# The order of small evictions in a fused attention and two-layer MLP kernel

## The chip, the cores and the metric

The kernel runs on one core of a Trainium2 chip. The metric is the device time of one execution in microseconds (us), the median over several runs. TensorE (PE in the profile) multiplies matrices into PSUM; VectorE (DVE), ScalarE (ACT) and GpSimd (POOL) work on tiles; SyncE (SP) issues the transfers. Each engine runs its own queue of instructions in order, and waits where an instruction needs another engine's result or has to leave a tile alone until another engine has read it.

## The reference

Causal attention with a decay, over 4 batches, 8 heads, 576 positions and 64 columns per head, and then two MLP layers over the 2304 tokens, all in float32:

```python
scores = scale * q @ k.T + decay                 # causal, per head
attn   = exp(scores - max) / (sum + 1e-9)
x      = (attn @ v) as 2304 tokens x 512
x      = (h - tanh(h)) @ w_out,   h = x @ w_in   # layer one, 512 -> 2048 -> 512
out    = relu(h)**2 @ w_out,      h = x @ w_in   # layer two, 512 -> 2048 -> 512
```

## The kernel before

**Numbers in two parts.** Most products are made from values split into a high part (fp32r, written by ScalarE) and a low part (the value minus its high part, written by VectorE). A product is then three matmul passes: high times high, high times low, low times high. So each value that PE reads first has one ScalarE instruction and one VectorE instruction behind it, and VectorE's can't begin before ScalarE's has ended.

**How the order is made.** A `Clockwork` object counts ticks. `cw.step(fn)` runs one piece of PE work and then whatever has come due; `cw.later(k, fn)` puts the eviction or split that follows on a heap, due k ticks later (the lags stand in `LAG`). What is written first has the higher priority, and a planner turns that into the queues of the engines. From the last block of layer one up to the tenth group of layer two, instructions that go through `pin` are kept strictly in the order in which they were written. The order in which instructions are written is also the order of the data: an instruction that writes a tile after another was written to read it waits for that read, and the other way round.

**Attention, second half.** The positions 256 to 575 of each head run as units n = 32 to 63, two neighbouring units (an even and an odd one) sharing a batch; PE alternates their pieces with matmuls of layer one. The softmax weights of a tile are turned by PE (`pt_atom`, L775), evicted as a high part into `PT[0]` (ACT, L784) three ticks later, and as a low part into `PT[1]` (DVE, L785) another two ticks later. `pv_atoms` then runs the product with the values in two passes: pass 0 reads `PT[0]` and pass 1 reads `PT[1]` (PE, L858). Both units of a pair use one copy of `PT[0]` and `PT[1]`, and they overlap in it: an odd unit's tile 2 lies where the even unit's tile 3 was.

**Last block of layer one.** Sixteen steps, each with 12 matmuls h (L1017) and 12 matmuls y (L1057) of 512 columns. An h is turned into g by a tanh (ACT, L1027), a difference (DVE, L1030), a high part (ACT, L1034) and a low part (DVE, L1038), and y of a step follows h of the next. Beside it the weights of layer two's first matrix are decoded, eight pieces p one after another (`decode_w`, `combine`, `split_all`); GpSimd makes sums of quarters (L256) and of inputs (L1186), and each piece has four splits, ACT high (L320) and DVE low (L321).

**Layer two's second matrix.** 36 groups n, each with 7 products of 6 matmuls (L1394). A group's inputs are loaded (`g_load`), squared (`g_square`, ACT L1336), combined by three differences and sums (`g_adds`, DVE L1344 to L1346) and split into a high part (`g_split`, ACT L1356) and a low part (`g_low`, DVE L1360), which PE reads. The table `AT` says before which product of group n the parts of a later group are written: before product 0 the high part of n + 2 and the differences of n + 3, then the low part of n + 2 before product 1, a load before product 3 and a square before product 5.

Of the kernel before, what the change touches and what calls it, by code (L numbers as in the profile page):

```python
# [10 lines left out]
F32 = mybir.dt.float32  # L11
# [3 lines left out]
ALU = mybir.AluOpType  # L15
# [3 lines left out]
B, H, S, D = 4, 8, 576, 64  # L19
NT, DM, DFF = B * S, H * D, 2048  # L20
P = 128
# [36 lines left out]
LAG = dict(max=2, exp=1, norm=3, tr=3, trlo=2, pv=1, pvadd=1, qk=1, qklo=1, th=1, sub=1, hi=1, lo=1, wbits=2, wparts=3,  # L58
           relu=1, sq=1, lo2=1, load=8)
# [51 lines left out]
def fused_kernel(ctx: ExitStack, tc: tile.TileContext, q, k, v, f, w1i, w1o, w2i, w2o, out):  # L111
    nc = tc.nc
# [33 lines left out]
    def pin(ins):  # L146
        if ordered:
            tc.keep_in_program_order(ins)
# [30 lines left out]
    def decoded():  # L179
        busy.pop()  # L180
        if pending:
            decode_w(*pending.pop(0))
# [130 lines left out]
    def split_all(phase, p, work, lag, at=None):  # L313

        def one(x):
            t, k, n, src = work[x]
            f = src.shape[-1]
            hi, lo = (t[:, hl, k : k + n].rearrange("p k f -> p (k f)").rearrange("p (c f) -> p c f", f=f)
                      for hl in range(2))
            pin(nc.scalar.activation(hi, src, AF.Copy))  # L320
            low = nc.vector.tensor_tensor(lo, in0=src, in1=hi.bitcast(F32), op=ALU.subtract)  # L321
            if phase == 2:
                pin(low)
            if x + 1 < len(work):
                if at is None:
                    cw.later(lag[x], lambda: one(x + 1))
            else:
                ready_w.add((phase, p))
                if phase == 1:
                    decoded()  # L330

        one(at or 0)

# [413 lines left out]
    def pt_atom(i):  # L747

        n, ts = slots[i]
        pb = Pb[i % RING]  # L750

        def a():
            while i not in ready_p:
                cw.step()
            if i == 0:
                keep_warm(WARM)
            t = bank("a", 4, f"pt_{i}")
            if len(ts) > 1:
                for x, (o, c) in enumerate(((0, 0), (128, 0), (128, 1))):
                    nc.tensor.transpose(t[:, x * P : x * P + P], pb[:, o + c * P : o + c * P + P], ident)  # L760
                cw.later(LAG['tr'], lambda: nc.scalar.activation(ptf(n), t[:, 0 : 3 * P], AF.Copy))
                return
            if not PT:
                for x in range(2):
                    PT.append(ap.tile([P, 1536], F32R, tag=f"PT{x}", name=f"PT{x}", bufs=1))
                PT.append(ap.tile([P, 2, P], F32R, tag="xq", name="PT4", bufs=1)[:, 0])
            ti = ts[0][0]
            if ti == 4:
                t4 = bank("a", 4, f"pt4_{i}")
                nc.tensor.transpose(t4[:, :P], pb[:, 512:640], ident)  # L770
                cw.later(LAG['tr'], lambda: last_keys(t4))
            nch = min(ti + 1, 4)
            for x in range(nch):
                s0 = (nch - 1 - x) * P
                nc.tensor.transpose(t[:, x * P : x * P + P], pb[:, s0 : s0 + P], ident)  # L775
            if ti == 4:
                src = t.rearrange("p (c h r) -> p c h r", c=4, h=2)
                dst = [each4(PT[x]) for x in range(2)]
            else:
                src = t[:, 0 : nch * P].rearrange("p (c r) -> p c r", c=nch)  # L780
                dst = [strided(PT[x], *PTC[n % 2][ti]) for x in range(2)]

            def ev():
                nc.scalar.activation(dst[0], src, AF.Copy)  # L784
                cw.later(LAG['trlo'], lambda: nc.vector.tensor_tensor(dst[1], src, dst[0].bitcast(F32), op=ALU.subtract))  # L785
            cw.later(LAG['tr'], ev)

        def last_keys(t4):
            nc.scalar.activation(PT[2], t4[:, :P], AF.Copy)
            x = PT[2][D:]  # L790
            cw.later(LAG['trlo'], lambda: nc.vector.tensor_tensor(x, t4[D:, :P], x.bitcast(F32), op=ALU.subtract))
        return 2 * sum((ti + 1) * rows for ti, rows, _, _ in ts), a

    def strided(t, d0, m):
# [3 lines left out]
    def each4(t):  # L798
        x = t[:, 0:D]
        return bass.AP(tensor=x.tensor, offset=x.offset, ap=[x.ap[0], [384, 4], [320, 2], [1, D]])  # L800

    ready_p = set()
    xs_box = {}
# [43 lines left out]
    def pv_atoms(n):  # L847
        b, hf, h = units[n]
        hh = h % 2
        nq = NQ[1]  # L850
        box = {}

        def a(hl):
            if hl == 0:
                box["t"] = bank("a", 4, f"pv_{n}")
            t = box["t"]
            for c, (c0, ql, w) in PVC[hh].items():
                nc.tensor.matmul(t[:, ql : ql + w], lhsT=VH[:, hh, c].rearrange("p a d -> p (a d)"),  # L858
                                 rhs=PT[hl][:, c0 : c0 + w], start=hl == 0 and c == 0, stop=False)
            if hl == 1:  # L860
                ql = 256 - 256 * hh
                nc.tensor.matmul(t[:, ql : ql + D], lhsT=VH[:, hh, 4].rearrange("p a d -> p (a d)"),
                                 rhs=PT[2][:, D - D * hh : 2 * D - D * hh], start=False, stop=True)
                cw.later(LAG['pv'], ev)

        def ev():
            t = box["t"]
            if hh == 0:
                xs_box["t"] = ap.tile([P, 320], F32, tag="xs", name=f"xs_{n}", bufs=2)
            xs = xs_box["t"]  # L870
            own = slice(hh * D, hh * D + D)
            oth = slice(D - hh * D, 2 * D - hh * D)
            tmp = ap.tile([P, 320], F32, tag="xtmp", name=f"xt_{n}", bufs=1)
            nc.scalar.activation(tmp[own, :nq], t[oth, :nq], AF.Copy)

            def fin():
                for c0, d0, w in ((0, 0, nq),) if hh == 0 else ((D, P, P), (D + P, 0, P), (0, 256, D)):
                    nc.vector.tensor_tensor(xs[own, d0 : d0 + w], t[own, c0 : c0 + w], tmp[own, c0 : c0 + w], op=ALU.add)
                if hh == 1:
                    pair_done(b, hf, h // 2, xs)  # L880
            cw.later(LAG['pvadd'], fin)

        cost = sum(max(256, w) for _, _, w in PVC[hh].values())
        return [(cost, lambda: a(0)), (cost + 256, lambda: a(1))]
# [230 lines left out]
    class Feed:  # L1115
# [11 lines left out]
        def one(self):  # L1127
            assert self.decoded < self.loaded
            decode_w(*self.items[self.decoded])
            self.decoded += 1  # L1130
# [138 lines left out]
    def put(g, dst):  # L1269
        move(dst, g.rearrange("p (b n) -> p b n", b=3))  # L1270

    def layer1():
        n = len(units1)
        for s in range(n):
            if s == 0:
                load_w(2, 0)
            if s < NP2:
                feed.upto(NF + s + 1)
            for pos, (d, k) in enumerate(STEP):
                if s == 0 and (d or k in PRE):  # L1280
                    continue
                due_at(7 * s + pos)
                cw.step(lambda: l1_product(s - d, k))
                feed.pace(NF + NP2)
        for at, (fn, x, k) in enumerate(((l2_product, 0, 1), (l2_product, 0, 6), (l1_product, n - 1, 4),
                                         (l2_product, 0, 7), (l1_product, n - 1, 3)), 7 * n):
            due_at(at)
            cw.step(lambda: fn(x, k))
# [45 lines left out]
    def g_square(n):  # L1334
        raw = graws[n][:, 0:4].rearrange("p k e t -> p (k e t)")
        pin(nc.scalar.activation(raw, raw, AF.Square))  # L1336
# [61 lines left out]
            cw.later(1, lambda: after2(j, k))  # L1398

    CALM = 10  # L1400
    AT = {0: ((g_split, 2), (g_adds, 3)), 1: ((g_low, 2),), 3: ((g_load, 5),), 5: ((g_square, 4),)}
    LATE = {(0, 4): (6, 0), (1, 4): (6, 1), (2, 4): (6, 2), (2, 6): (7, 0), (3, 4): (7, 1), (4, 2): (7, 2)}
    tmp2, outs2 = {}, {}
# [43 lines left out]

    def layer2():
        third()
        g_square(3)  # L1450
        g_load(4)
        g_load(5)
        for n in range(NG):
            if n == CALM:
                ordered.clear()
            for x, k in enumerate(ORDER2):
                for fn, m in AT.get(x, ()):
                    if n + m < NG and (fn is not g_square or n + m > 3) and (fn is not g_load or n + m > 5):
                        fn(n + m)
                if (n, x) in LATE:  # L1460
                    final_piece(*LATE[n, x])
                if n == 0 and x < 3:
                    continue
                cw.step(lambda: l2_product(n, k))
# [93 lines left out]
```

## Time and profile before

| | us |
|---|---|
| median of 3 runs (lowest to highest) | 1010.33 (1009.06 to 1011.22) |
| the profiled execution | 1005.81 |
| its span | 1004.1 |
| PE busy | 977.4 |
| DVE busy | 722.0 |
| ACT busy | 627.1 |
| POOL busy | 356.3 |

The span is the stretch from the first to the last instruction of the profiled execution. Busy is the time in which an engine had an instruction running; the ends of matmuls are modelled, so that neighbouring matmuls overlap a little in the rows.

### The profile page before, as it was taken

Reading aid. Unit: us, or ns where it says so; the run is one execution under the profiler, and the core shown is the slowest. Engines: PE = TensorE matmul, PEld = TensorE weight load, DVE = VectorE, ACT = ScalarE, POOL = GpSimd, SP = SyncE. Lnnn points to the kernel's source line nnn. Section 1 sums busy time; section 2 is a strip of 40 time slices with the busy share of each in tenths; the row PEclk is TensorE's granted clock in tenths of the full one; section 3 lists DMA queues with packets and bytes.
Section 4 is the critical chain, followed back from the end, with each engine's and each line's share of the span. In section 5 each row is a group of like instructions: output and inputs, shape, how many; then the busy total and the mean of one; then the engine's idle time right before and its main releaser. Section 6 shows DMA issues by size and latency. Waiting matters only on the chain.

```text
span 1004.1 us, 19916 instructions
## 1 busy us (share of the span) xinstructions
PE 977.4 (97%) x6990; PEld 929.5 (93%) x6990; DVE 722.0 (72%) x1513; ACT 627.1 (62%) x1249; POOL 356.3 (35%) x511
## 2 busy tenths in 40 slices
PE   7989999999999999999999999999999999999998
PEld 5778889999999999999999877999999999999998
DVE  4897884587878877878753589755447569987773
ACT  5896874566666666665643367767666767655551
POOL 4664453455566655565510343342323000000000
PEclk9999999999999999999999999999999999999999
DMA  8946744363353444443201432576877974544431
GB/s 235 272 137 228 217 112 100 107 140 82 101 142 91 115 120 102 113 120 93 75 20 36 153 127 84 162 258 222 282 272 247 331 229 118 168 141 134 127 106 42
DMA packets 220004, 149.58 MB, mean 149 GB/s; under 512 B 116384, under 2 KB 197600, under 8 KB 219904
## 3 DMA queue, kind: packets, MB, share of 16 engines
q1 hardware_dynamic: 219856, 148.28, 50.3%
q8 instruction: 55, 0.90, 0.4%
q14 instruction: 45, 0.37, 0.1%
q10 hardware_dynamic: 48, 0.03, 0.0%
HBM read 101.00 MB, written 39.92 MB: 140 GB/s over the span
## 4 chain that ended last, share of the span: by engine, by line
PE 68%; DVE 10%; ACT 3%; issue 2%; DMA 1%; SPq 1%; POOL 1%; DVEq 0%; ACTq 0%; POOLq 0%
PE o L1394 17%; PE r L1226 15%; PE h L1017 14%; PE y L1057 14%; PE pv L858 3%; PE pt L775 2%; DVE KL L630 2%; PE s L740 2%; DVE PT L785 2%; PE s L742 1%; DVE Pb L669 1%; DVE g L1030 1%; DVE ghl L1038 1%; DVE wq L321 1%; PE pv L820 1%
## 5 line engine op out<-in xcount | busy, mean ns | idle before, releaser
L1057 PE MATMUL y<-ghl,w 128*128 128x256 f32 (+1 forms) x1536 | 241.2, 301 | 1.5 <-DVE ghl L1038 1.5
L1057 PEld LDWEIGHTS y<-ghl,w 128*128 128x128 f32 x1536 | 209.5, 191 | 13.4 <-DVE ghl L1038 3.3
L1017 PE MATMUL h<-x,w 128*128 128x256 f32 x1344 | 199.2, 291 | 5.5 <-POOL w L228 4.7
L1017 PEld LDWEIGHTS h<-x,w 128*128 128x128 f32 x1344 | 175.9, 192 | 12.8 <-POOL w L228 6.3
L1394 PE MATMUL o<-ws,gc 128*128 128x256 f32 x864 | 116.0, 283 | 0.0
L1394 PEld LDWEIGHTS o<-ws,gc 128*128 128x128 f32 x864 | 109.2, 192 | 0.0
L1226 PE MATMUL r<-yt,ws 128*128 128x384 f32 x576 | 106.6, 336 | 0.5 <-ACT g L1244 0.5
L1226 PEld LDWEIGHTS r<-yt,ws 128*128 128x128 f32 x576 | 100.0, 188 | 2.9 <-ACT g L1244 2.5
L1394 PE MATMUL o<-wq,gc 128*128 128x256 f32 x648 | 90.9, 284 | 1.7 <-DVE gc L1360 1.5
L694 POOL TENSOR_SCALAR Pb<-Pb,st 128x384 f32<-128x384 f32 (+2 forms) x80 | 58.0, 726 | 81.1 <-DVE st L688 60.7
L1394 PEld LDWEIGHTS o<-wq,gc 128*128 128x128 f32 x648 | 83.5, 192 | 2.5 <-DVE gc L1360 1.9
L669 DVE CUSTOM_DVE_ANT_0 Pb<-s,Pb 128x128 f32<-128x128 f32 (+4 forms) x144 | 66.9, 482 | 22.1 <-PE s L742 13.8
L678 ACT ACTIVATE Pb<-Pb,st 128x384 f32<-128x384 f32 (+2 forms) x80 | 55.2, 689 | 42.8 <-DVE st L669 42.0
L1226 PE MATMUL r<-yt,wq 128*128 128x384 f32 x432 | 80.1, 335 | 0.3 <-ACT g L1244 0.2
L1030 DVE TENSOR_TENSOR g<-h,g 128x512 f32<-128x512 f32 x72 | 49.4, 686 | 42.5 <-ACT g L1027 41.8
L1360 DVE TENSOR_TENSOR gc<-graw,gc 128x1792 fp32r<-128x1792 f32 x34 | 68.7, 2022 | 13.5 <-ACT gc L1356 13.5
L1226 PEld LDWEIGHTS r<-yt,wq 128*128 128x128 f32 x432 | 75.1, 188 | 1.3 <-ACT g L1244 1.1
L1356 ACT ACTIVATE gc<-graw 128x1792 fp32r<-128x1792 f32 x34 | 57.7, 1697 | 28.0 <-PE o L1394 17.6
L256 POOL TENSOR_TENSOR wsum<-wfull 128x256 f32<-128x256 f32 x32 | 29.9, 935 | 118.5 <-DVE wfull L212 95.3
L1237 DVE TENSOR_TENSOR g<-r,g 128x384 f32<-128x384 f32 x71 | 39.0, 553 | 42.3 <-PE r L1226 23.3
L1027 ACT ACTIVATE g<-h 128x512 f32<-128x512 f32 x72 | 42.7, 592 | 40.2 <-PE h L1017 39.6
L1034 ACT ACTIVATE ghl<-g 128x512 fp32r<-128x512 f32 x72 | 45.4, 630 | 34.6 <-DVE g L1030 33.9
(155 smaller groups left out, 1879.1 us busy)
## 6 DMA issues: line engine op xcount, KB each, us to landing
graw<-gscr SPq DMA_DIRECT2D x144, 128.0 KB, 2.6
gscr<-g SPq DMA_DIRECT2D x95, 192.0 KB, 3.6
wraw<-in_moe_w_in_dram SPq DMA_DIRECT2D x32, 512.0 KB, 4.6
wraw<-in_moe_w_out_dram SPq DMA_DIRECT2D x32, 512.0 KB, 5.5
neg<-cscr SPq DMA_DIRECT2D x32, 288.0 KB, 3.4
v<-in_v_dram SPq DMA_DIRECT2D x48, 128.0 KB, 2.8
qk<-in_k_dram SPq DMA_DIRECT2D x64, 72.0 KB, 2.4
K<-K SPq DMA_DIRECT2D x32, 144.0 KB, 3.0
```

The costliest lines, as they stand in the source:

```text
L669: nc.vector.tensor_tensor_reduce(out=d, in0=t[:rows, src : src + m], in1=d, scale=-0.125, scalar=3.0e38 if j == 0 else stat(0, x)[:rows], ...
L678: nc.scalar.activation(d, d, AF.Exp, bias=stat(len(parts) - 1, x)[:rows], scale=-1.0, accum_out=stat(2, x)[:rows])
L694: nc.gpsimd.tensor_scalar(d, d, r, 1.0, op0=ALU.mult, op1=ALU.mult)
L1017: nc.tensor.matmul(o, lhsT=win(fc, wh, dc), rhs=xpart(j, dc, xh), start=dc == 0 and wh + xh == 0, stop=dc == ND - 1 and wh == 1)
L1027: pin(nc.scalar.activation(g, t, AF.Tanh))
L1030: pin(nc.vector.tensor_tensor(g, t, g, op=ALU.subtract))
L1034: pin(nc.scalar.activation(ghl[:, 0], g, AF.Copy))
L1057: nc.tensor.matmul(o, lhsT=wout(fc, wh, i * P, P), rhs=ghl[:, xh, fj * n : fj * n + n], start=s == 0 and fj == 0 and wh + xh == 0 and i % ...
L1226: nc.tensor.matmul(t, lhsT=wprod(1, p, k, wh)[:, dc * P : (dc + 1) * P], rhs=yt[i, k][:, xh, dc], start=k in FRESH and dc == 0 and wh + xh ...
L1356: pin(nc.scalar.activation(hi, t[:, 1:8], AF.Copy))
L1360: pin(nc.vector.tensor_tensor(lo, in0=t[:, 1:8], in1=hi.bitcast(F32), op=ALU.subtract))
L1394: nc.tensor.matmul(o, lhsT=gc[n][gh, e][:, GWHERE[k]] if n == 1 else gc[n][gh][:, GWHERE[k], e], rhs=wprod(2, 2 * q + e, k, wh), start=q = ...
```

## The change

It has three parts.

1. In the second half of attention, an eviction of turned weights is written only once the pass that reads the same buffer for the unit before it has been written (`behind`), and a pass is written only once all evictions that it reads have been (the loop over `need`, which lets ticks go by without PE work).
2. In layer two's opening groups, a table `OPEN` replaces `AT` for n = 0 and 1: `g_square(3)` moves from ahead of the loop to behind `g_split(2)`; `g_adds(3)` moves behind `g_low(2)`; `g_square(4)` and `g_adds(4)` move behind `g_low(3)`.
3. In the last block, the low parts of layer two's first weights are written two ticks after their high parts instead of together with them, and are pinned; the piece counts as ready, and the next one's decoding begins, behind its last low part. From layer two's first products on they are written at once as before.

```diff
@@ split_all
             pin(nc.scalar.activation(hi, src, AF.Copy))
-            low = nc.vector.tensor_tensor(lo, in0=src, in1=hi.bitcast(F32), op=ALU.subtract)
-            if phase == 2:
-                pin(low)
-            if x + 1 < len(work):
-                if at is None:
-                    cw.later(lag[x], lambda: one(x + 1))
+            if x + 1 < len(work) and at is None:
+                cw.later(lag[x], lambda: one(x + 1))
+
+            def low():
+                pin(nc.vector.tensor_tensor(lo, in0=src, in1=hi.bitcast(F32), op=ALU.subtract))
+                if x + 1 == len(work):
+                    ready_w.add((phase, p))
+                    if phase == 1:
+                        decoded()
+            if phase == 1 and not units_on:
+                cw.later(2, low)
             else:
-                ready_w.add((phase, p))
-                if phase == 1:
-                    decoded()
+                low()
@@ pt_atom
-                cw.later(LAG['tr'], lambda: last_keys(t4))
+                cw.later(LAG['tr'], lambda: behind(n, 1, lambda: last_keys(t4, n)))
...
             def ev():
                 nc.scalar.activation(dst[0], src, AF.Copy)
-                cw.later(LAG['trlo'], lambda: nc.vector.tensor_tensor(dst[1], src, dst[0].bitcast(F32), op=ALU.subtract))
-            cw.later(LAG['tr'], ev)
+                split_done[0].add((n, ti))
+                cw.later(LAG['trlo'], lambda: behind(n, 1, low))
+
+            def low():
+                nc.vector.tensor_tensor(dst[1], src, dst[0].bitcast(F32), op=ALU.subtract)
+                split_done[1].add((n, ti))
+            cw.later(LAG['tr'], lambda: behind(n, 0, ev))
...
+    def behind(n, hl, fn):
+
+        if n == NH0 or (n - 1, hl) in valued:
+            fn()
+        else:
+            cw.later(1, lambda: behind(n, hl, fn))
@@ pv_atoms
+            need = {(n - hh, 4), (n, 2), (n, 3)} | ({(n - hh, "last")} if hl else set())
+            while not need <= split_done[hl]:
+                cw.step()
+            valued.add((n, hl))
@@ layer1
+        units_on.append(True)
@@ layer2
+    OPEN = ({0: ((g_split, 2), (g_square, 3)), 1: ((g_low, 2),), 2: ((g_adds, 3),)},
+            {0: ((g_split, 2),), 1: ((g_low, 2),), 2: ((g_square, 3),), 3: ((g_adds, 3), (g_load, 5)), 5: ((g_square, 4),)})
...
-        g_square(3)
         g_load(4)
         g_load(5)
...
-                for fn, m in AT.get(x, ()):
-                    if n + m < NG and (fn is not g_square or n + m > 3) and (fn is not g_load or n + m > 5):
+                for fn, m in (OPEN[n] if n < 2 else AT).get(x, ()):
+                    if n + m < NG:
                         fn(n + m)
```

## Rows read from the trace of the kernel before

**Rows 1.** The page's busy time by engine, with shares of the span and instructions.

```profile
PE 977.4 (97%) x6990; PEld 929.5 (93%) x6990; DVE 722.0 (72%) x1513; ACT 627.1 (62%) x1249; POOL 356.3 (35%) x511
```

**Rows 2.** Waits of PE over the span: us in total, times, longest us.

```profile
PE pv L858 <- DVE PT L785: 4.4, 6, 1.1
PE y L1057 <- DVE ghl L1038: 1.5, 2, 0.9
PE o L1394 <- DVE gc L1360: 1.5, 2, 0.8
...
PE o L1394 <- ACT gc L1356: 0.3, 1, 0.3
```

**Rows 3.** Timeline, passes of unit 34: start us, us, engine, line, [idle before <- releaser].

```profile
219.37 1.62 PE L1017 MATMUL h<-x,w 128*128 128x256 f32 x12
...
219.62 0.68 DVE L785 TENSOR_TENSOR PT<-pt,PT 128x512 fp32r<-128x512 f32 x1
...
220.41 0.49 ACT L784 ACTIVATE PT<-pt 128x384 fp32r<-128x384 f32 x1 [1.59 <-DVE st L688]
220.94 0.56 DVE L785 TENSOR_TENSOR PT<-pt,PT 128x384 fp32r<-128x384 f32 x1
221.55 0.80 PE L858 MATMUL pv<-PT,VH 128*128 128x320 f32 x4 [0.57 <-DVE PT L785]
...
222.90 0.48 DVE L878 TENSOR_TENSOR xs<-pv,xt 64x320 f32<-64x320 f32 x1 [1.41 <-ACT xt L874]
```

**Rows 4.** PE's timeline, the passes of unit 35 and the second pass of unit 60.

```profile
229.87 1.62 PE L1017 MATMUL h<-x,w 128*128 128x256 f32 x12
231.33 0.69 PE L858 MATMUL pv<-PT,VH 128*128 128x320 f32 x4
...
494.85 0.80 PE L858 MATMUL pv<-PT,VH 128*128 128x320 f32 x4 [0.55 <-DVE PT L785]
```

**Rows 5.** Timeline, the first pass of the last unit, 63.

```profile
518.26 0.63 ACT L1034 ACTIVATE ghl<-g 128x512 fp32r<-128x512 f32 x1 [0.38 <-DVE g L1030]
...
518.89 0.70 PE L858 MATMUL pv<-PT,VH 128*128 128x320 f32 x4
...
519.62 0.60 ACT L784 ACTIVATE PT<-pt 128x512 fp32r<-128x512 f32 x1 [0.73 <-PE pv L858]
```

**Rows 6.** Timeline, the last block around the first piece's low parts.

```profile
572.08 2.88 PE L1017 MATMUL h<-xl,w 128*128 128x512 f32 x12
...
576.43 3.84 POOL L1186 TENSOR_TENSOR yr<-yr,yr 128x768 f32<-128x768 f32 x2
...
577.51 2.88 PE L1017 MATMUL h<-xl,w 128*128 128x512 f32 x12
...
578.58 2.25 DVE L321 TENSOR_TENSOR ws<-wsum,ws 128x512 fp32r<-128x512 f32 x1 [1.22 <-ACT ws L320]
...
581.35 0.68 DVE L321 TENSOR_TENSOR ws<-wsum,ws 128x512 fp32r<-128x512 f32 x1
581.48 2.79 PE L1057 MATMUL y<-ghl,w 128*128 128x512 f32 x11 [0.86 <-DVE ghl L1038]
...
584.11 2.88 PE L1017 MATMUL h<-xl,w 128*128 128x512 f32 x12
```

**Rows 7.** Timeline, the opening of layer two's second matrix.

```profile
821.10 0.43 DVE L1346 TENSOR_TENSOR graw<-graw 128x256 f32<-128x256 f32 x1
...
823.63 1.06 ACT L1336 ACTIVATE graw<-graw 128x1024 f32<-128x1024 f32 x1 [3.06 <-DMA graw<-gscr]
...
824.59 1.68 ACT L1356 ACTIVATE gc<-graw 128x1792 fp32r<-128x1792 f32 x1
...
826.31 2.03 DVE L1360 TENSOR_TENSOR gc<-graw,gc 128x1792 fp32r<-128x1792 f32 x1
...
828.39 0.74 PE L1394 MATMUL o<-wq,gc 128*128 128x256 f32 x4 [0.84 <-DVE gc L1360]
...
829.31 1.06 ACT L1336 ACTIVATE graw<-graw 128x1024 f32<-128x1024 f32 x1 [2.09 <-DMA graw<-gscr]
```

More of the change, by code (lines that the diff above doesn't have):

```diff
@@ L784, in ev, with last_keys, low @@
                 nc.scalar.activation(dst[0], src, AF.Copy)
-                cw.later(LAG['trlo'], lambda: nc.vector.tensor_tensor(dst[1], src, dst[0].bitcast(F32), op=ALU.subtract))
-            cw.later(LAG['tr'], ev)
-        def last_keys(t4):
+                split_done[0].add((n, ti))
[4 more added lines that the diff above has]
+            cw.later(LAG['tr'], lambda: behind(n, 0, ev))
+        def last_keys(t4, n):
             nc.scalar.activation(PT[2], t4[:, :P], AF.Copy)
             x = PT[2][D:]
-            cw.later(LAG['trlo'], lambda: nc.vector.tensor_tensor(x, t4[D:, :P], x.bitcast(F32), op=ALU.subtract))
+            def low():
+                nc.vector.tensor_tensor(x, t4[D:, :P], x.bitcast(F32), op=ALU.subtract)
+                split_done[1].add((n, "last"))
+            cw.later(LAG['trlo'], low)
         return 2 * sum((ti + 1) * rows for ti, rows, _, _ in ts), a
@@ L800, in each4 @@
         return bass.AP(tensor=x.tensor, offset=x.offset, ap=[x.ap[0], [384, 4], [320, 2], [1, D]])
+    split_done, valued = (set(), set()), set()
+    def behind(n, hl, fn):
[3 more added lines that the diff above has]
+            cw.later(1, lambda: behind(n, hl, fn))
     ready_p = set()
@@ L1270, in put @@
         move(dst, g.rearrange("p (b n) -> p b n", b=3))
+    units_on = []
     def layer1():
+        units_on.append(True)
         n = len(units1)
```

## The prediction

> **What bounds the kernel now.** I read the busy times first: PE is busy for 97% of the span [rows 1], so the kernel is PE's work plus the few moments in which PE stands still. Then the waits of PE, and in them only those that a part of the change touches [rows 2]: the value passes wait for a low part (4.4 us, 6 times), y in the last block waits for g's low part (1.5 us, twice), and layer two's products wait for a group's low and high parts (1.5 and 0.3 us). That is 7.7 us of idle PE. Then the timeline of each place, to see who is late and why [rows 3 to 7].
>
> PE loses more at a wait than its idle time. Twelve matmuls of 256 columns ahead of a pass take 1.46 us from start to start when nothing waits (231.33 minus 229.87) [rows 4]; where the second pass of unit 34 waited they took 2.18 us (221.55 minus 219.37) [rows 3]. The loss is 0.72 us, the row's idle time 0.57: add 0.15 us to each such wait. In the last block a round took 5.43 us undisturbed (572.08 to 577.51) and 6.60 us with the wait (577.51 to 584.11), so 1.17 us were lost where the row says 0.86: add 0.3 us [rows 6].
>
> **Part 1, the turned weights.** Count ticks in the old code for units 34 to 39 and 50 to 55: the odd unit's low part of tile 2 is due in the same tick as the even unit's second pass and is written just ahead of it. Both touch one region of PT[1]. So the second pass of the even unit reads what the odd unit wrote, and waits for it. The row shows that chain: unit 34's last low part ends at 220.30, the odd unit's high part starts at 220.41 (it may not overwrite PT[0] sooner), its low part runs 220.94 to 221.50, and the pass starts at 221.55 [rows 3]. In the other ten pairs the even pass is written first. Six pairs have this order, and six waits are counted [rows 2], but not one to one: the wait of 0.55 us at 494.85 is unit 60's, whose order is right, and it stays [rows 4]; the sixth wrong pair hides its chain behind other matmuls. Five waits go: 4.4 - 0.55 = 3.85 us, plus 5 x 0.15 = 4.6 us. After the change unit 34's pass needs only the low part that ends at 220.30, while PE would reach it at about 219.37 + 1.46 = 220.83: no wait is left, by half a microsecond.
>
> What is late next is the odd unit's low part, which must now wait until the pass has read PT[1]. It is one DVE instruction of 0.56 us, and queued behind it are the eviction of the pass's result and the next tile's maximum. In the row DVE stood idle 1.41 us before that eviction [rows 3], so the wait has room; I cost it at nothing, and at up to 0.5 us a pair, 3 us in all, if that room is gone.
>
> One place gets a wait. The last unit's first pass is written one tick before its own last high part, so the pass now has to let that one go first. The pass started at 518.89; the eviction takes 0.60 us and may stand behind the ACT instruction that ends at 518.89 [rows 5]. The cost is between 0 and 0.7 us; I take 0.5. Part 1 gives 4.6 - 0.5 = 4.1 us, between 1.6 and 5.
>
> **Part 3, the last block.** For the first piece the old order on DVE is: two low parts, g's difference, a low part, g's low part, a low part. The third low part stands ahead of g's low part, and it waits 1.22 us for ACT, which makes its high part only after g's, and then takes 2.25 us, against 0.68 us for the same instruction at 581.35 [rows 6]. With two more ticks, and the lags as they stand, the order is g's difference, two low parts, g's low part, the other two. For the third piece (the second of the two waits, 1.5 - 0.86 = 0.64 us) all four low parts fall behind g's. Both waits would go: 1.5 + 2 x 0.3 = 2.1 us.
>
> The long 2.25 us lie beside two GpSimd instructions, 576.43 to 580.27 [rows 6], and DVE was done 0.56 us after they ended: it didn't share with them, it stood. The Trainium skill (SBUF — State Buffer, "SBUF: two separate sides") says that a VectorE instruction with two SBUF inputs and a GpSimd instruction that reads SBUF take one port pair in turn, the first to start holding it for its whole length; the trace agrees. By that rule part 3 would give 0.5 us less than 2.1, since g's low part has two SBUF inputs as well.
>
> Worked out from the rows: g's low part, wherever it is put, can't run before 580.27 if GpSimd keeps its place, and takes 0.68 us; it would end near 580.95 instead of 581.43. PE then gains about 0.5 of the first 1.17 us. I take 1.6 us for part 3. The bounds are 0 (another low part is caught in the same way) and 2.1. Each piece is two ticks longer, so the decoding of the last ones slides into layer two's first products by some five ticks; their weights are needed tens of ticks later, so nothing waits for it. No transfer moves.
>
> **Part 2, the opening of layer two.** Group 2's differences are done at 821.53, yet its high part starts at 824.59, because ACT's queue holds group 3's square ahead of it, which waits 3.06 us for its load; and its low part starts at 826.31, since DVE then makes group 3's differences (about 1.6 us) first. PE waits 0.84 us for it at 828.39 [rows 7], after 0.3 us for the high part [rows 2]. In the new order the high part runs 821.6 to 823.3 and the low part to 825.4, before PE asks at about 826.1. Group 3's square comes at 823.63 with its load as before, its differences at 825.4 to 827.0, its high part to 828.7, its low part to 830.7; PE, 42 matmuls or 5.1 us after 826.1, asks at 831.2. Group 3's wait, the other 0.7 us of the 1.5, goes as well. Sum: 1.5 + 0.3 + 3 x 0.15 = 2.2 us.
>
> What is late next is group 4: its square can't run before its load has landed, at 829.31 as before [rows 7]. Its differences end at 832.3, group 5's go ahead of its low part (the table from n = 2 on is the old one), and the low part ends near 836.7, where PE, now 2 us earlier, asks for it at 836.4. I take 0.4 us off: 1.8 us, between 0.9 (group 4 gives back the second wait whole) and 2.2.
>
> **The sum.** 4.1 + 1.6 + 1.8 = 7.5 us of the profiled execution: 1005.81 becomes 998.3, its span 1004.1 becomes 996.6. The median of the runs lies 4.5 us above the profiled execution; the same 7.5 us off it give 1002.8 us, 0.74% faster. A difference of 0.2%, 2 us, is about what a measurement here can tell from none.
>
> **The rivals.**
> - *The wait only moves to DVE (chance 0.13).* The odd unit's low part blocks DVE until the pass is done, and what stands behind it makes PE wait a few pieces later. Against it: 1.41 us of idle DVE behind that instruction [rows 3], and ten pairs that already run so with one wait of 0.55 us [rows 4]. With 3 us given back the time is 1005.8.
> - *The port decides the last block (0.12).* GpSimd holds one low part after another, both waits of y stay, and part 3 is worth nothing: 1004.4.
> - *The change doesn't do what it says (0.10).* The planner, not the written order, had set these queues, and five of the seven waits come back elsewhere: 1009 to 1010. Against it: the places of the waits are those that the written order gives.
> - *Slower (0.05).* The old dependence kept the even units' second passes back. With it gone the planner may put each of them straight behind the first pass, ahead of the 12 matmuls between (1.46 us), before the unit's low part is there: at unit 34 the low part ends 0.9 us after the first pass makes room (220.30 against 219.37) [rows 3]. On all 16 even units that costs up to 16 x (0.9 + 0.15) = 17 us and PE gains only 7.5: 1020. It decides once more than seven units are moved so.
> - *As forecast (0.60).* 1002.8, itself between 1000.5 and 1004.5.
>
> **How the numbers follow.** If every loss goes and nothing is given back, 4.6 + 2.1 + 2.2 = 8.9 us give 1001.4; the runs shown spread by 1 us to each side, so the range begins at 1000. It takes in the first two rivals and ends at 1007.5; the other two, 0.15, lie outside, with a little of the forecast's own. Faster by over 0.2%: forecast and the first two rivals, 0.85. Within 0.2%: 0.10. Slower: 0.05.
>
> **What would show it.** The waits of the value passes fall from six to one or two and their total to about 0.6 us; the even units' second passes start right after the matmuls ahead of them; DVE shows short waits for PE ahead of the odd units' low parts. In the last block every round takes 5.4 to 5.6 us. In layer two, the high part of group 2 starts near the end of its differences, and what wait is left is group 4's. The prediction is wrong if the order of PE's work in attention differs from before in more than the units named, if g's low part in the last block still follows a stalled low part, or if the opening's transfers land later.

## The result, and the profile after

The changed kernel took 999.4 us (median of 4 runs, 998.31 to 1002.03) against 1010.25 us for the kernel before (4 runs, 1009.06 to 1011.22): a ratio of 0.9916, with an interval of 0.9891 to 0.9941. Measured again in a later session, beside the experiments, it took 1003.42 us (9 runs, 1000.2 to 1006.36) against 1009.71 us, a ratio of 0.9939 [0.9919, 0.9958]. The first median lies 0.6 us below the forecast range, the second 0.6 us above the forecast 1002.8; the median of all 13 runs is 1001.9. Faster it is, by 0.6% to 0.8%.

The page of the changed kernel, busy time by engine (its profiled execution took 1002.03 us, its span is 1000.3):

```profile
PE 977.9 (98%) x6990; PEld 932.5 (93%) x6990; DVE 721.4 (72%) x1513; ACT 628.5 (63%) x1249; POOL 358.8 (36%) x511
```

The work is the same as in [rows 1], to the instruction; only the idle time has changed. The waits of PE in the changed kernel, of the value passes, of y and of layer two (us in total, times, longest):

```profile
PE r L1251 <- ACT g L1265: 1.6, 1, 1.6
PE y L1082 <- DVE ghl L1063: 1.4, 2, 0.9
...
PE pv L883 <- DVE PT L792: 0.6, 1, 0.6
...
PE pv L883 <- ACT PT L787: 0.5, 2, 0.2
PE r L1251 <- ACT g L1269: 0.4, 1, 0.4
```

Against [rows 2]: the passes' 4.4 us have become 0.6, the second matrix's 1.5 and 0.3 are gone altogether (no wait at L1422 is left), and the passes' waits for high parts have grown from 0.2 to 0.5 us. y has two waits again, but one of them, 0.86 us, is at 62 us, far ahead of the last block, where only 0.53 is left. New is the first line: 1.6 us for g in layer two's first products. That is a wait which the change made.

**Where the time went.** The two spans differ by 3.8 us, the medians by 10.9, so one must look by stage. A stage's length is read from the first and last start of a line's instructions. For the changed kernel (the line of the value passes, of layer two's first products r, of its second matrix o: ns min/median/max, then first and last start):

```profile
L883 PE MATMUL pv<-PT,VH x256: 249/308/417, 203.2 to 520.7; 128*128 128x320 f32 x128
...
L1251 PE MATMUL r<-yt,wq x432: 333/334/445, 632.0 to 815.0; 128*128 128x384 f32 x144
...
L1422 PE MATMUL o<-wq,gc x648: 278/283/284, 812.7 to 996.0; 128*128 128x256 f32 x162
```

and for the kernel before, the value passes alone:

```profile
L858 PE MATMUL pv<-PT,VH x256: 249/308/417, 198.8 to 521.5; 128*128 128x320 f32 x128
```

The first 199 to 203 us, ahead of the first pass, are work that the change doesn't touch, and yet they are 4.4 us longer in this execution; more on that at the end. What lies behind it is shorter as a whole: 805.3 us before, 797.1 after. By stage, in us, for all kernels of this study (worked out from such lines of each; names of experiments as below; the kernel before had medians of 1009.63, 1009.71 and 1007.71 us in the three sessions of the experiments, each on a chip of its own, and each ratio is within a session):

| kernel | to the first pass | passes, first to last | last pass to first r | first r to first o | o, first to last | median, ratio to before [95%] |
|---|---|---|---|---|---|---|
| before | 198.8 | 322.7 | 113.1 | 179.2 | 186.0 | |
| changed | 203.2 | 317.5 | 111.3 | 180.7 | 183.3 | 999.4, 0.9916 [0.9891, 0.9941] |
| changed, again | 200.9 | 317.5 | 111.4 | 181.7 | 183.4 | 1003.42, 0.9939 [0.9919, 0.9958] |
| part 1 alone | 199.7 | 317.5 | 113.1 | 179.6 | 185.6 | 1004.9, 0.9953 [0.9934, 0.9972] |
| part 2 alone | 200.9 | 322.7 | 113.1 | 178.7 | 183.3 | 1005.78, 0.9972 [0.9955, 0.9989] |
| part 3 alone | 205.6 | 322.7 | 111.2 | 182.3 | 185.8 | 1010.29, 1.0009 [0.9989, 1.003] |
| parts 1 and 2 | 205.0 | 317.5 | 113.2 | 180.5 | 183.4 | 1004.07, 0.9935 [0.9914, 0.9956] |
| decoding on time | 204.5 | 317.6 | 112.1 | 179.3 | 183.4 | 1001.77, 0.9923 [0.9895, 0.9952] |
| differences later | 202.3 | 317.6 | 110.7 | 181.9 | 183.4 | 1000.97, 0.9921 [0.9896, 0.9947] |
| both | 203.6 | 317.5 | 112.2 | 177.9 | 183.4 | 999.11, 0.9908 [0.988, 0.9936] |
| mixed | 203.0 | 317.5 | 111.9 | 178.9 | 183.3 | 1000.35, 0.9929 [0.9905, 0.9954] |
| no wait for the eviction | 202.9 | 317.5 | 111.2 | 180.9 | 183.4 | 1001.91, one run |

Read down a column: the passes' stage has two lengths, 322.7 and 317.5, and which one depends on part 1 alone. The last column of stages goes from about 185.8 to 183.4 with part 2. The third goes from 113.1 to 111.3 with part 3, and the fourth gets longer with it.

**Unit 34 in the changed kernel** (timeline: start us, us, engine, line, then idle time before and what ended it), against [rows 3]:

```profile
223.75 1.62 PE L1042 MATMUL h<-x,w 128*128 128x256 f32 x12
...
224.00 0.68 DVE L792 TENSOR_TENSOR PT<-pt,PT 128x512 fp32r<-128x512 f32 x1
...
224.80 0.49 ACT L787 ACTIVATE PT<-pt 128x384 fp32r<-128x384 f32 x1 [1.59 <-DVE st L691]
...
225.21 0.69 PE L883 MATMUL pv<-PT,VH 128*128 128x320 f32 x4
...
225.92 0.56 DVE L792 TENSOR_TENSOR PT<-pt,PT 128x384 fp32r<-128x384 f32 x1 [0.65 <-PE pv L883]
...
226.46 0.48 DVE L903 TENSOR_TENSOR xs<-pv,xt 64x320 f32<-64x320 f32 x1
```

The even unit's low part ends at 224.68, the 12 matmuls take 1.46 us from start to start, and the second pass starts at 225.21 without a wait. The odd unit's low part now waits 0.65 us for it, and the eviction behind that follows without a gap: DVE's idle time has only moved.

**The last unit's first pass** (PE's timeline, the passes of units 62 and 63), against [rows 5]:

```profile
513.75 0.69 PE L883 MATMUL pv<-PT,VH 128*128 128x320 f32 x4
...
518.56 0.80 PE L883 MATMUL pv<-PT,VH 128*128 128x320 f32 x4
...
520.28 0.69 PE L883 MATMUL pv<-PT,VH 128*128 128x320 f32 x4
```

**The last block**, the first piece, against [rows 6]:

```profile
575.40 4.10 POOL L1211 TENSOR_TENSOR yr<-yr,yr 128x768 f32<-128x768 f32 x2
575.53 4.26 DVE L325 TENSOR_TENSOR wq<-wfull,wq 128x512 fp32r<-128x512 f32 x2
...
579.71 0.68 DVE L1063 TENSOR_TENSOR ghl<-g,ghl 128x512 fp32r<-128x512 f32 x1
...
580.45 2.80 PE L1082 MATMUL y<-ghl,w 128*128 128x512 f32 x11 [0.53 <-DVE ghl L1063]
```

The two low parts ahead of g's stand beside GpSimd's differences for 4.26 us, and end 0.29 us after them; g's low part ends at 580.39, and y waits 0.53 us instead of 0.86.

**Layer two's first products**, where nothing waited in the forecast:

```profile
644.31 0.63 ACT L320 ACTIVATE ws<-wsum 128x512 fp32r<-128x512 f32 x1 [1.05 <-POOL wsum L256]
...
645.19 0.63 ACT L320 ACTIVATE ws<-wsum 128x512 fp32r<-128x512 f32 x1 [0.25 <-POOL wsum L256]
645.73 0.66 ACT L203 ACTIVATE wfull<-wraw 128x512 uint32<-128x512 uint32 x1
646.28 0.65 ACT L204 ACTIVATE wfull<-wraw 128x512 f32<-128x512 f32 x1
646.83 0.52 ACT L1265 ACTIVATE g<-g 128x384 f32<-128x384 f32 x1
647.25 0.65 ACT L203 ACTIVATE wraw<-wraw 128x512 uint32<-128x512 uint32 x1
647.80 0.65 ACT L204 ACTIVATE wraw<-wraw 128x512 f32<-128x512 f32 x1
648.36 0.47 ACT L1265 ACTIVATE g<-r 128x384 f32<-128x384 f32 x1
648.88 0.62 PE L1251 MATMUL r<-yt,wq 128*128 128x384 f32 x2 [1.55 <-ACT g L1265]
```

From 644.31 on ACT makes the high parts of a late piece (the seventh) and begins the decoding of the next (L203, L204), all in the written order; two relus of r's results (L1265) stand between and behind them, and PE waits 1.55 us until the second has read its bank of r. On the way ACT stands still for 1.3 us itself, waiting for GpSimd's sums of the late piece (L256). The kernel before made the last high part of the same piece here:

```profile
634.61 2.27 PE L1226 MATMUL r<-yt,wq 128*128 128x384 f32 x12
...
642.03 0.63 ACT L320 ACTIVATE ws<-wsum 128x512 fp32r<-128x512 f32 x1 [0.30 <-POOL wsum L256]
```

That is 7.4 us after the first r (634.61). In the changed kernel it is 13.1 us (645.19, with the first r at 632.05): the piece has slid by 5.7 us.

**The opening of the second matrix**, against [rows 7]:

```profile
820.00 0.42 DVE L1374 TENSOR_TENSOR graw<-graw 128x256 f32<-128x256 f32 x1
820.54 1.70 ACT L1384 ACTIVATE gc<-graw 128x1792 fp32r<-128x1792 f32 x1 [1.07 <-DVE graw L1374]
822.27 2.02 DVE L1388 TENSOR_TENSOR gc<-graw,gc 128x1792 fp32r<-128x1792 f32 x1 [1.85 <-ACT gc L1384]
...
828.35 1.06 ACT L1364 ACTIVATE graw<-graw 128x1024 f32<-128x1024 f32 x1 [0.72 <-DMA graw<-gscr]
...
833.25 2.02 DVE L1388 TENSOR_TENSOR gc<-graw,gc 128x1792 fp32r<-128x1792 f32 x1
```

Group 2's high part starts 0.12 us after its differences (820.42), where it lost 3.06 us before. Group 4's square still waits for its load, and its low part ends at 835.27; PE waits for neither.

### The profile page after: what moved, and what is told of

It reads as the page before. It is cut to its first block, busy times and chain, and to the rows that moved or that the text cites. A ratio compares the mean times of both kernels' runs of the same rounds, so it can differ in the third digit from the quotient of the medians.

```text
span 1000.3 us, 19927 instructions
## 1 busy us (share of the span) xinstructions
PE 977.9 (98%) x6990; PEld 932.5 (93%) x6990; DVE 721.4 (72%) x1513; ACT 628.5 (63%) x1249; POOL 358.8 (36%) x511
## 4 chain that ended last, share of the span: by engine, by line
PE 74%; DVE 5%; ACT 3%; issue 2%; DMA 1%; POOL 1%; SPq 0%; ACTq 0%; DVEq 0%; POOLq 0%
PE o L1422 18%; PE h L1042 16%; PE y L1082 16%; PE r L1251 13%; PE pv L883 3%; PE pt L778 2%; PE s L743 2%; PE s L745 1%; DMA wscr<-wfull 1%; DVE KL L633 1%; DVE PT L792 1%; DVE Pb L672 1%; PE pv L841 1%; DVE ghl L1063 0%; ACT Pb L681 0%
## 5 line engine op out<-in xcount | busy, mean ns | idle before, releaser
L1422 PE MATMUL o<-ws,gc 128*128 128x256 f32 x864 | 116.5, 283 | 0.0
L1422 PEld LDWEIGHTS o<-ws,gc 128*128 128x128 f32 x864 | 109.4, 192 | 0.0
L1422 PE MATMUL o<-wq,gc 128*128 128x256 f32 x648 | 90.6, 283 | 0.0
L1422 PEld LDWEIGHTS o<-wq,gc 128*128 128x128 f32 x648 | 83.5, 192 | 0.0
L256 POOL TENSOR_TENSOR wsum<-wfull 128x256 f32<-128x256 f32 x32 | 30.5, 954 | 120.3 <-DVE wfull L212 101.1
L1063 DVE TENSOR_TENSOR ghl<-g,ghl 128x512 fp32r<-128x512 f32 x72 | 54.8, 762 | 14.6 <-ACT ghl L1059 14.1
```

What stands on the lines that cost most here:

```text
L1063: pin(nc.vector.tensor_tensor(ghl[:, 1], g, ghl[:, 0].bitcast(F32), op=ALU.subtract))
L1422: nc.tensor.matmul(o, lhsT=gc[n][gh, e][:, GWHERE[k]] if n == 1 else gc[n][gh][:, GWHERE[k], e], rhs=wprod(2, 2 * q + e, k, wh), start=q = ...
```

## The experiments

**Each part alone.** The kernel before with one part of the diff each: the order of the turned weights, the table of the opening, the late low parts.

```diff
# part 1 alone
+                cw.later(LAG['trlo'], lambda: behind(n, 1, low))
+            cw.later(LAG['tr'], lambda: behind(n, 0, ev))
+            while not need <= split_done[hl]:
+                cw.step()
# part 2 alone
-        g_square(3)
+                for fn, m in (OPEN[n] if n < 2 else AT).get(x, ()):
# part 3 alone
+            if phase == 1 and not units_on:
+                cw.later(2, low)
```

> The kernel before with part 1 alone (the order of the evictions of turned weights). Theory: the stretch from the first to the last value pass takes 5.2 us less, as in the changed kernel's profile (322.7 to 317.5 us), five of PE's six waits for low parts of turned weights are gone, and nothing after it changes: about 5 us faster than before. Rival: the wait only moves to VectorE and comes back as other waits of PE in attention; then 2 us or less.

> The kernel before with part 2 alone (layer two's opening groups). Theory: the stretch from layer two's first product to the last takes 2.7 us less, PE waits nowhere in it, and the kernel is about 2.5 us faster. Rival of the prediction: group 4 gives 0.4 us or more of the 2.2 back, since its square's load lands no sooner; then 1.8 us or less, with a wait of PE at group 4.

> The kernel before with part 3 alone (low parts two ticks later in the last block). Theory: the last block gains about 1.8 us, and 1.5 us go again in one wait of PE (1.6 us) in layer two's first products, since the decoding of the pieces has slid; the kernel is 0 to 0.5 us faster, that is the same. Rival, as the prediction had it: 1.6 us faster and no such wait.

Part 1 alone gave 4.7 us of the median and 5.2 us of its stage, part 2 alone 3.9 us and 2.7 us, part 3 alone nothing that can be measured: its stage became 1.9 us shorter, and the next one 3.1 us longer. PE's waits in the kernel with part 3 alone:

```profile
PE r L1229 <- ACT g L1247: 1.8, 2, 1.0
...
PE r L1229 <- ACT g L1243: 1.6, 1, 1.6
PE y L1060 <- DVE ghl L1041: 0.5, 1, 0.5
```

Here the last block has the one wait of y that the changed kernel has, and the 1.6 us for g at L1243 (the changed kernel's L1265) stand there too, with neither of the other parts in it.

**All but the late low parts.** Parts 1 and 2, beside the changed kernel measured again.

```diff
# against the changed kernel
-            if phase == 1 and not units_on:
-                cw.later(2, low)
-            else:
-                low()
+            low()
```

> The changed kernel with part 3 undone (parts 1 and 2 alone). Theory: parts 1 and 2 are all of the gain, some 8 us, within 0.5 us of the changed kernel. Rival: part 3 carries 1.6 us of the gain, and this kernel is that much slower than the changed one.

> The changed kernel once more, beside the others on one chip. Theory by stretches of its first profile: 8.2 us faster than the kernel before (ratio 0.9918), the first 200 us being the same program. Rival by the first median: 10.9 us (ratio 0.9893).

Without part 3 the ratio is 0.9935, with it 0.9939: what it is worth, either way, is less than these runs can tell. (The repetition's own 0.9939 met neither of its two expectations, 0.9918 and 0.9893; its profiled execution is 7.1 us shorter than the kernel before behind the first pass, not 8.2.) The wait for g at the line of the changed kernel's L1265 is in all five kernels with part 3 as it stands (1.5 to 1.65 us: changed, again, part 3 alone, differences later, no wait for the eviction) and in none of the others. The stage from first r to first o is 179.2, 179.6, 178.7 and 180.5 without part 3, mean 179.5, and 180.7, 181.7, 182.3, 181.9 and 180.9 with it, mean 181.5: on the mean 2.0 us are given back of the 1.9 gained, 1.5 to 1.65 of them in that wait. The last high part of the seventh piece comes 13.0 to 13.2 us after the first r in these five kernels, and 7.3 to 7.4 us after it in all others.

**Is it the lateness of the decoding, and who makes the long low parts?** Two edits of the changed kernel. In the first the next piece's decoding begins with the last high part, so that it isn't put off, while the low parts stay two ticks late. In the second GpSimd's second pair of differences of inputs is written two steps later, away from the first piece's low parts. Then both.

```diff
# decoding on time
+            late = phase == 1 and not units_on
...
-                    if phase == 1:
+                    if phase == 1 and not late:
                         decoded()
...
                 cw.later(2, low)
+                if x + 1 == len(work):
+                    decoded()
# differences later
-    SUMMED, SPLIT = (3, 4, 6, 7), (5, 6, 8, 9, 11, 13, 15)
+    SUMMED, SPLIT = (3, 4, 8, 9), (5, 6, 8, 9, 11, 13, 15)
```

> The changed kernel, but the decoding of the next piece begins with the last high part, as before the change; only the low parts stay two ticks late. Theory: the wait of 1.55 us at layer two's first products (PE for ScalarE's g, at 648.88 us of the changed kernel) comes from the decoding that had slid into them; it goes, the stretch from layer two's first product to its second matrix's first falls from 180.7 to about 179.2 us, and the last block stays at 111.3 us: 1.5 us faster than the changed kernel. Rival: that wait comes from the late low parts themselves or from the last outputs of layer one; then it stays.

> The changed kernel, but GpSimd's third and fourth differences of inputs are written two steps later (before steps 8 and 9 of the last block instead of 6 and 7). Theory: the two low parts that took 4.26 us beside them (575.53 us of the changed kernel) were held by GpSimd; alone they take some 1.2 us, PE's remaining wait of 0.53 us in the last block goes, and the stretch from the last value pass to layer two's first product falls from 111.3 to about 110.5 us. Rival: GpSimd's sums of quarters hold VectorE just as long, or the differences hold the next piece's low parts at their new place; then the wait stays or moves.

> The two edits together on the changed kernel. Theory: the gains add up, some 2.3 us faster than the changed kernel, about 10.5 us faster than the kernel before (ratio near 0.9895). Rival: one of the two waits was hiding the other; then 1.5 us or less.

With the decoding on time the 1.6 us for g are gone, and the stage of the first products is 179.3 us again. The low parts are still two ticks late and pinned there, so neither of these makes the wait. The last block keeps only 1.0 of its 1.9 us, where the expectation had it keep all: y waits twice in it, 0.9 us in all. With the differences later the first piece's low parts look like this (DVE's timeline):

```profile
574.67 1.01 DVE L325 TENSOR_TENSOR wq<-wfull,wq 128x512 fp32r<-128x512 f32 x2
575.60 0.69 DVE L1063 TENSOR_TENSOR ghl<-g,ghl 128x512 fp32r<-128x512 f32 x1
```

The pair that took 4.26 us takes 1.01, no wait of y is left, and the stage is the shortest of all, 110.7; but the late decoding is still there, and the next stage takes 181.9. The moved differences hold g's low part of a later step there, but only one low part (0.92 us) stands ahead of it, and it comes in time (the same timeline):

```profile
586.39 2.33 DVE L1063 TENSOR_TENSOR ghl<-g,ghl 128x512 fp32r<-128x512 f32 x1
```

With both, the pieces run earlier: two low parts stand ahead of g's low part of that step, the moved differences hold the pair and then g's low part, and y waits (that kernel's timeline):

```profile
586.82 2.69 DVE L326 TENSOR_TENSOR wq<-wfull,wq 128x512 fp32r<-128x512 f32 x2
586.93 4.29 POOL L1214 TENSOR_TENSOR yr<-yr,yr 128x768 f32<-128x768 f32 x2
...
589.43 2.33 DVE L1066 TENSOR_TENSOR ghl<-g,ghl 128x512 fp32r<-128x512 f32 x1
...
591.82 1.43 PE L1085 MATMUL y<-ghl,w 128*128 128x512 f32 x5 [0.61 <-DVE ghl L1066]
```

Here y waits twice, 1.0 us in all. The two edits therefore don't add up in the last block (112.2), but the first products fall to 177.9, and the kernel is the fastest of the study: 999.11 us, 4.3 us under the changed kernel in the same session, whose runs overlap with its own. Fitted as at the end of this text, at equal clock, it is 2.5 us under it, give or take 1.2.

**A mixture**, meant to have the good side of each: the first two pieces put the decoding off as in the changed kernel, the others don't.

```diff
# against the kernel with both
+            soon = phase == 1 and not units_on and p >= 2
...
-                    if phase == 1 and not late:
+                    if phase == 1 and not soon:
                         decoded()
```

> The changed kernel with GpSimd's differences two steps later, and with the decoding of the next piece begun with the last high part only from the third piece on; the first two pieces begin it behind their last low part. Theory (what a late piece costs is paid in layer two's first products, and four ticks of lateness are too few for that; what is gained by lateness is that the moved differences don't meet g's low part of that step at the moment when y needs it): from the last value pass to the first product of layer two 110.7 to 111.2 us, from there to the second matrix 178 to 179.5 us, no wait of y in the last block over 0.3 us, no wait of layer two's products for g over 0.5 us; the time is 0.5 to 1.5 us below the kernel with both edits. Rival (any lateness at all is handed on to the first products): the second stage is 180 to 182 us, with a wait of about 1.5 us for g, and the time is that of the kernel with the later differences alone.

It missed: the stage of the first products is 178.9, as the theory had it, but the last block took 111.9, not 110.7 to 111.2. Its one wait of y, in PE's timeline:

```profile
607.99 2.79 PE L1086 MATMUL y<-ghl,w 128*128 128x512 f32 x11 [0.82 <-DVE ghl L1067]
```

It isn't the moved differences that hold g's low part up there, but one of GpSimd's sums (1.05 us from 606.34; the low part runs 1.22 us from 606.71). Four ticks more or less decide which GpSimd instruction the low parts meet, and 0.5 to 0.8 us with it. Nor does this kernel show that layer two's first products bear four ticks of lateness: its seventh piece comes 7.4 us after the first r, as in the kernel before, so that the lateness of the first two pieces was gone by then. Against the kernel with both it is 0.6 us slower at equal clock, give or take 1.2: undecided.

**The wait of the last unit.** The changed kernel without the loop over `need`: as before the change, the last unit's first pass then runs ahead of its own last high part.

```diff
-            while not need <= split_done[hl]:
-                cw.step()
```

> The changed kernel without the loop that holds a value pass back until the evictions that it reads have been written: part of the last unit's first product is made from weights that another unit left in the buffer. Theory (that wait costs little, since the second pass follows sooner): unit 63's first pass starts 4.2 to 4.4 us after unit 62's second, as before the change, its second pass 2.0 to 2.2 us behind it, and the stretch from the first to the last value pass is 317.2 to 317.5 us, 0 to 0.3 us shorter than in the changed kernel. Rival (the forecast's 0.5 us): the stretch is 317.0 us or less, and the second pass comes 1.7 us behind the first.

Its passes (PE's timeline, units 62 and 63):

```profile
513.46 0.69 PE L881 MATMUL pv<-PT,VH 128*128 128x320 f32 x4
...
517.72 0.70 PE L881 MATMUL pv<-PT,VH 128*128 128x320 f32 x4
...
519.83 0.80 PE L881 MATMUL pv<-PT,VH 128*128 128x320 f32 x4
```

From the second pass of 62 the first of 63 starts 4.26 us later, its second another 2.11 us: 6.37 us. In the changed kernel it is 4.81 and 1.72, together 6.53. So the wait delays the first pass by 0.55 us, as forecast, and the second by 0.16 us; PE fills the gap with matmuls that stood between the two.

## Why the prediction was right, and where it was wrong

The direction and the size were right, 7.5 us forecast. Behind the first pass the profiled changed kernel is 8.2 us shorter (805.3 less 797.1), measured again 7.1. But the sum owes that to luck: two terms were too small (by 1.1 and 0.9 us), one was too large (by 1.6), and the errors nearly cancel.

- **Part 1: right, under-sized.** Forecast 4.1, measured 5.2 us of stage. Just the five waits named went, the sixth stayed where it was said to stay. From first to second pass, units 34, 36, 38, 50 and 52 took 0.73, 1.02, 1.08, 0.74 and 1.30 us less, together 4.87, for 3.84 us of idle time: the surcharge of 0.15 us a wait, taken from unit 34 alone, was 0.21 on the mean. Unit 54, the pair that was said to hide its chain behind other matmuls, gained 0.26 nonetheless: no idle time in the rows isn't no cost. And the last unit cost 0.16, not 0.5, since the price was taken from the delay of the first pass alone. The odd units' low parts wait as forecast, and nothing came of it: the rival of the moved wait is refuted. So is the one by which the written order doesn't set the queues, since the five waits didn't come back elsewhere, and so is the slower one: the even units' second passes still stand behind the matmuls that were ahead of them, and PE's order in attention differs only beside unit 38 (two matmuls h) and at the last unit.
- **Part 2: right, under-sized.** Forecast 1.8, measured 2.7 (186.0 to 183.3). The three waits of 1.8 us were 2.7 us of time, again more per wait than the surcharge. The 0.4 us to be given back at group 4 didn't come: its differences ended at 831.20, as worked out (832.3, less the 1.1 us by which o began earlier), but group 5's differences and the low part behind them took 4.07 us, not 4.4, and there was no wait of PE.
- **Part 3: wrong, in its last step.** Forecast 1.6, measured nothing. The last block gained 1.9 us (1.6 was said), with the one wait of y left that the forecast left there. That total fits better than its parts: 0.3 us came from the first wait (0.5 was said), 0.9 from the second, and 0.6 from three rounds in which no wait had been counted. One round still takes 6.28 us, not 5.4 to 5.6, and by one of the forecast's own signs this part was wrong: g's low part does follow stalled low parts, the pair of 4.26 us. What made the part worth nothing lies behind the block, though. What failed is the sentence that the decoding of the last pieces slides "into layer two's first products by some five ticks; their weights are needed tens of ticks later, so nothing waits for it". Nobody waits for the weights, indeed. But the decoding is pinned in ACT's queue in the written order, and slid by 5.7 us it stands ahead of relus that empty the banks of r, which PE does wait for: 1.55 us at one place, 2.0 us of the stage's mean. The kernel with the decoding on time shows the cause: low parts just as late behind their high parts, no slide, no such wait. How the wait grows with the slide isn't shown, since every kernel of this study has either the whole slide at that place or none.
- **The port.** That GpSimd's differences and DVE's low parts stand in each other's way was forecast, and shown by moving one of them: 4.26 us for the pair beside the differences, 1.01 us without, and 2.33 us instead of 0.69 for g's low part where they were moved to. The Trainium skill (SBUF — State Buffer, "SBUF: two separate sides") says that the one who starts first holds the port pair for its whole instruction; these rows agree. As a rival (both waits of y stay, and part 3 is worth nothing for this reason) it is refuted: one wait went, the block gained, and the loss came elsewhere; the 0.53 us that is left there is the port's.
- **The range.** 1000 to 1007.5 was laid around the median shown, 4.5 us above the profiled execution. The two sessions of the changed kernel differ by 4 us in median, as much as half the effect, and their mean granted clocks, 0.993 and 0.990, go with most of that (below).

Open is why the stage of the first products varies by 1 to 2 us among kernels that don't differ in it (178.7 to 180.5 without part 3); the wait for g at L1269 in the changed kernel's numbering, 0.4 us there and 1.5 us in the same kernel measured again, has a part in it.

## What to carry to other kernels

A wait for data may be a wait for the order in which instructions were written: look whether the tile that is waited for is one that the reader needs, or one that a later writer has overwritten too soon; here, taking five such waits away cost 0.16 us at one other place. When a step is put off, ask not only who needs its result, but whose instructions it now stands in front of in the queue of every engine that it uses. And judge a change of less than one per cent by stage: here one stage alone, which the change doesn't touch, varied by 6.8 us, more than any of the change's three parts was worth.

## What the runs showed of the hardware

The first 200 us run the same instructions, PE's and GpSimd's in the same order, in the kernel before and the changed one, and no edit of the study lies in them; they took 198.8 to 205.6 us. The granted clock goes with it. Windows of 5 us in the changed kernel (start:end, length, busy time of each engine, then PEclk, DMA share, GB/s):

```profile
55.00:60.00 5.00, 2.48 (x15) 1.63 (x14) 5.00 (x7) 5.00 (x13) 4.51 (x5) 1.00 0.00 0
85.00:90.00 5.00, 5.00 (x29) 5.00 (x29) 2.06 (x5) 3.06 (x6) 0.72 (x2) 0.60 0.40 89
110.00:115.00 5.00, 5.00 (x26) 5.00 (x25) 2.98 (x10) 2.51 (x7) 2.47 (x4) 0.50 1.04 305
```

and in the kernel with part 3 alone, where another such place was:

```profile
45.00:50.00 5.00, 5.00 (x27) 5.00 (x27) 4.41 (x16) 3.08 (x11) 0.00 (x0) 0.54 0.87 255
```

0.50 is 1.2 GHz throughout, 1.00 is 2.4 GHz, and 0.60 and 0.54 hold both. In these low windows PE was busy all the time, and the half-idle one, at 55 to 60 us, ran at 1.00; but it isn't always so. The same window of the kernel before, with PE busy for 3.28 of its 5 us:

```profile
55.00:60.00 5.00, 3.28 (x15) 2.67 (x16) 5.00 (x7) 4.09 (x11) 3.37 (x3) 0.79 0.00 0
```

Between 40 and 130 us, from what the windows lack to 1.00, the clock was at the lower level for about 10 us in the kernel before, 14 us in the changed one and 20 us in the one with part 3 alone; in the first 40 us, where the mean clock was 1.00, 0.96 and 0.91, for none, 3 and 7 us. Their first stages are 198.8, 203.2 and 205.6 us. Why it falls in one execution and not in the next isn't shown. Over the whole span the mean clock of the kernel before was between 0.986 and 0.995 in 62 timed runs, and its time between 1004.31 and 1013.11 us. A line fitted through all 146 timed runs of this study, one level for each kernel and one common slope, gives 7.7 us for 0.01 of clock (give or take 0.7) and leaves a scatter of 1.2 us. At equal clock it puts the changed kernel 7.4 us under the kernel before by its first four runs (give or take 1.2, where the medians differ by 10.9) and, measured again, 6.9 us, part 1 alone 5.2, part 2 alone 2.5, parts 1 and 2 together 7.2, part 3 alone 0.6 above it (each give or take 0.8), and the kernel with both edits 9.4 under it (give or take 1.0): near the stages' sums, by another way.
